# Scores of q and of grad_out in PSUM tiles of their own, and exp one slot earlier, in a decode attention with its gradients

## The chip, the cores and the metric

One core of a Trainium2 chip. The metric is the device time of one execution in microseconds (us), the median of the timed runs. "TensorE" (PE in the profile) does the matmuls and transposes, "VectorE" (DVE) and "ScalarE" (ACT) the elementwise work, "GpSimd" (POOL) issues the stores, "SyncE" (SP) the loads. 16 DMA engines move the data between HBM and SBUF.

## The reference

For 64 heads (2 x 32) there is one query q of 128 numbers, 8192 keys k and values v of 128 numbers each, and the gradient grad_out of the output. All are bf16. What is computed is the output of attention and its three gradients:

```python
def fwd(q, k, v):
    scores = jnp.einsum("bhqd,bhkd->bhqk", q, k) * D ** -0.5
    p = softmax(scores, axis=-1)
    return jnp.einsum("bhqk,bhkd->bhqd", p, v)

out, vjp = jax.vjp(fwd, q, k, v)
return (out, *vjp(grad_out))          # out, dq, dk, dv
```

k and v are read (2 MB a head each), dk and dv are written (2 MB a head each). For each head: s = k q and dp = v grad_out are two columns of 8192 numbers; p is the softmax of the scaled s; dS = p (dp - sum(p dp)); dk is dS times q and dv is p times grad_out, row by row.

## The kernel before, in words

A head's k and v lie in SBUF as 64 tiles (NT) of 128 rows, so that 8192 keys are 128 partitions x 64 columns. They are handled in chunks of 16 tiles (CH): four chunks of k, then four of v, so that a head has eight slots (SL). The main loop (L344) goes through the slots of 64 heads and two more heads' worth of slots for what lags behind, 528 in all; `pin` keeps the instructions of each engine in the order in which they are written.

In slot s of head i TensorE gets this, in this order: 16 transposes of chunk s into a PSUM tile `tp` (L144), which ScalarE copies to SBUF as `ev` (L146, 128 x 2048); 16 matmuls of the head before, which accumulate its output from v (slots 0 to 3, L276, `oacc`) or its dq from k (slots 4 to 7, L292, `qacc`); and 16 matmuls of one column each that give the scores of the chunk of the slot before from its `ev` (L156). The first four chunks give s, the last four dp.

Between these stand the few steps of the softmax. After the scores of chunk 3, in slot 4, VectorE takes the maximum of s by partition (L168, `mp`); in slot 5 TensorE transposes it (L172, into mT) and VectorE takes the maximum of all (L174, `gm`); in slot 6 TensorE spreads it over the partitions (L178, into mb) and VectorE scales it (L181, `negm`). In slot 7, behind the copy of chunk 7, ScalarE computes exp (L191, `E_f`, with the row sums), and VectorE casts it (L201, `E_bf`), which the matmuls of L276 need in slot 0 of the next head. In slot 0 of the next head VectorE multiplies E_f with dp and sums (L207), in slot 1 the sums are spread (L221, into lsum) and dS is made (L243).

VectorE's large work is the outer products (L324, `ob`), four pieces of dv and four of dk a head, which lag by one to two heads. When `ob` is full GpSimd issues its store (L336).

The buffers: kt and vt have three each, so the load of v of head i+1 (L111) waits until the accumulation L276 of head i-2 is done, and the load of k (L106) until L292 of head i-2 is done. `ob` has two for dk and two for dv. In PSUM, `tp` has two buffers, `ps_m` two. `sdpw` (L131) is one tile of 64 + 64 + 128 + 1 + 2 fp32 columns in one bank, with two buffers, and holds s, dp, mT, mb and lsum of a head side by side. The framework puts in a wait wherever an instruction writes a tile that another engine still reads, by the tile and not by its columns.

Of the kernel before, what the change touches and what calls it, by code (L numbers as in the profile page):

```python
# [12 lines left out]
F32 = mybir.dt.float32  # L13
# [5 lines left out]
def kernel(  # L19
# [14 lines left out]
    P = nc.NUM_PARTITIONS  # L34
# [3 lines left out]
    NT = Sk // P  # L38
    assert NT * P == Sk and NT == 4 * CH
    NCH = NT // CH  # L40
# [10 lines left out]
    work = ctx.enter_context(tc.tile_pool(name="work", bufs=3))  # L51
    outp = ctx.enter_context(tc.tile_pool(name="outp", bufs=2))
    ps_tp = ctx.enter_context(tc.tile_pool(name="ps_tp", bufs=2, space=bass.MemoryType.PSUM))
    ps_sdp = ctx.enter_context(tc.tile_pool(name="ps_sdp", bufs=2, space=bass.MemoryType.PSUM))
    ps_m = ctx.enter_context(tc.tile_pool(name="ps_m", bufs=2, space=bass.MemoryType.PSUM))


# [24 lines left out]

    dqT = const.tile([P, BH], BF16)
    o_all = const.tile([1, BH, D], BF16)

    MT0 = 2 * NT
    MB0 = MT0 + P
    LS0 = MB0 + 1
    SDPW = LS0 + 2

    class Head:
        pass
# [1 line left out]
    heads = [Head() for _ in range(BH)]  # L94

    def load_k(i):
        h = heads[i]
        h.kt = kvp.tile([P, NT, D], BF16, tag="K", name="kt")
        if i == 0:
            for c in range(NCH):  # L100
                load_eng.dma_start(
                    out=h.kt[:, c * CH : (c + 1) * CH, :],
                    in_=k_v[i, :, c * CH : (c + 1) * CH, :],
                )
        else:
            load_eng.dma_start(out=h.kt[:], in_=k_v[i])  # L106

    def load_v(i):
        h = heads[i]
        h.vt = kvp.tile([P, NT, D], BF16, tag="V", name="vt")  # L110
        load_eng.dma_start(out=h.vt[:], in_=v_v[i])  # L111

    def broadcast(i):

        h = heads[i]
        qbp = ps_m.tile([P, 2, D], F32, tag="m", name="qbp")
        pin(
            nc.tensor.matmul(  # L118
                qbp[:],
                lhsT=ident_bf[:BH, i : i + 1].to_broadcast([BH, P]),  # L120
                rhs=qd_nat[:],
                start=True,
                stop=True,
            )
        )
        h.qb = work.tile([P, 2, D], BF16, tag="qb", name="qb")
        pin(nc.vector.tensor_copy(out=h.qb[:], in_=qbp[:]))  # L127

    def begin(i):
        h = heads[i]  # L130
        h.sdpw = ps_sdp.tile([P, SDPW], F32, tag="sdp", name="sdpw")  # L131
        h.s = h.sdpw[:, 0:NT]
        h.dp = h.sdpw[:, NT : 2 * NT]
        h.mT = h.sdpw[0:1, MT0 : MT0 + P]
        h.mb = h.sdpw[:, MB0 : MB0 + 1]
        h.lsum = h.sdpw[:, LS0 : LS0 + 2]

    def transpose_chunk(i, c):
        h = heads[i]
        src = h.kt if c < NCH else h.vt  # L140
        n0 = (c % NCH) * CH
        tp = ps_tp.tile([P, CH, P], BF16, tag="tp", name="tp")
        for t in range(CH):
            pin(nc.tensor.transpose(tp[:, t, :], src[:, n0 + t, :], ident_bf[:]))  # L144
        ev = evp.tile([P, CH, P], BF16, tag="ev", name="ev")
        pin(nc.scalar.copy(out=ev[:], in_=tp[:]))  # L146
        return ev

    def score_chunk(i, c, ev):
        h = heads[i]  # L150
        w = c // NCH
        dst = h.s if w == 0 else h.dp
        n0 = (c % NCH) * CH
        for t in range(CH):
            pin(
                nc.tensor.matmul(  # L156
                    dst[:, n0 + t : n0 + t + 1],
                    lhsT=ev[:, t, :],
                    rhs=qdT[:, w, i : i + 1],
                    start=True,  # L160
                    stop=True,
                )
            )

    def max_part(i):
        h = heads[i]
        h.mp = work.tile([P, 1], F32, tag="mp", name="mp")
        pin(nc.vector.reduce_max(out=h.mp[:], in_=h.s, axis=AX.X))  # L168

    def max_all(i):  # L170
        h = heads[i]
        pin(nc.tensor.transpose(h.mT, h.mp[:], ident_f[:]))  # L172
        h.gm = work.tile([1, 1], F32, tag="gm", name="gm")
        pin(nc.vector.reduce_max(out=h.gm[:], in_=h.mT, axis=AX.X))  # L174

    def max_spread(i):
        h = heads[i]
        pin(nc.tensor.matmul(h.mb, lhsT=ones_f[0:1, :], rhs=h.gm[:], start=True, stop=True))  # L178
        h.negm = work.tile([P, 1], F32, tag="negm", name="negm")
        pin(  # L180
            nc.vector.tensor_scalar(  # L181
                out=h.negm[:], in0=h.mb, scalar1=-scale, scalar2=None, op0=ALU.mult
            )
        )

    def expo(i):
        h = heads[i]
        h.E_f = work.tile([P, NT], F32, tag="E_f", name="E_f")
        h.ld = work.tile([P, 2], F32, tag="ld", name="ld")
        pin(  # L190
            nc.scalar.activation(  # L191
                out=h.E_f[:],
                in_=h.s,
                func=ACT.Exp,
                bias=h.negm[:],
                scale=scale,
                accum_out=h.ld[:, 0:1],
            )
        )
        h.E_bf = work.tile([P, NT], BF16, tag="E_bf", name="E_bf")  # L200
        pin(nc.vector.tensor_copy(out=h.E_bf[:], in_=h.E_f[:]))  # L201

    def weigh(i):
        h = heads[i]
        junk = work.tile([P, NT], BF16, tag="junk", name="junk")
        pin(
            nc.vector.tensor_tensor_reduce(  # L207
                out=junk[:],
                in0=h.E_f[:],
                in1=h.dp,  # L210
                scale=1.0,
                scalar=0.0,
                op0=ALU.mult,
                op1=ALU.add,
                accum_out=h.ld[:, 1:2],
            )
        )
# [51 lines left out]
    def acc_o(i, c):  # L269

        h = heads[i]
        if c == 0:
            h.oacc = ps_m.tile([1, D], F32, tag="m", name="oacc")
        for n in range(c * CH, (c + 1) * CH):
            pin(
                nc.tensor.matmul(  # L276
                    h.oacc[:],
                    lhsT=h.E_bf[:, n : n + 1],
                    rhs=h.vt[:, n, :],
                    start=(n == 0),  # L280
                    stop=(n == NT - 1),
                )
            )

    def acc_dq(i, c):

        h = heads[i]
        if c == 0:
            h.qacc = ps_m.tile([P, 1], F32, tag="m", name="qacc")
        for n in range(c * CH, (c + 1) * CH):  # L290
            pin(
                nc.tensor.matmul(  # L292
                    h.qacc[:],
                    lhsT=h.kt[:, n, :],
                    rhs=h.dS_bf[:, n : n + 1],
                    start=(n == 0),
                    stop=(n == NT - 1),
                )
            )

    def end_o(i):
        h = heads[i]
        pin(
            nc.scalar.activation(  # L304
                out=o_all[:, i, :], in_=h.oacc[:], func=ACT.Copy, scale=h.rl[0:1, :]
            )
        )

    def end_dq(i):
        h = heads[i]  # L310
        pin(
            nc.scalar.activation(
                out=dqT[:, i : i + 1], in_=h.qacc[:], func=ACT.Copy, scale=h.rls[:]
            )
        )
# [28 lines left out]
    for g in range(SL * (BH + 2)):  # L344
        i, s = divmod(g, SL)
        live = i < BH
        one = 0 <= i - 1 < BH
        two = 0 <= i - 2 < BH
        if s == 0 and i + 1 < BH and i >= 1:
            load_v(i + 1)  # L350
            load_k(i + 1)
        if live:
            if s == 0:
                begin(i)
            if s == 1:
                broadcast(i)
            ev = transpose_chunk(i, s)

        if live and s == 5:
            max_all(i)  # L360
        if live and s == 7:
            expo(i)
        if one and s == 1:
            normalise(i - 1)
        if one:
            if s < NCH:
                acc_o(i - 1, s)
            else:
                acc_dq(i - 1, s - NCH)
        if live and s == 6:  # L370
            max_spread(i)
        if prev is not None:
            score_chunk(*prev)
        prev = (i, s, ev) if live else None
        if live and s == 4:
            max_part(i)
        if one and s == 0:
            weigh(i - 1)
        if one and s == NCH - 1:
            end_o(i - 1)  # L380
        if one and s == SL - 1:
            end_dq(i - 1)
        if one and 2 <= s < 6:
            outer(i - 1, 1, s - 2)
        if one and s >= 6:
            outer(i - 1, 0, s - 6)
        if two and s < 2:
            outer(i - 2, 0, s + 2)
# [37 lines left out]
```

## Time and profile before

| what | us |
|---|---|
| median of the 2 timed runs | 1506.98 (1506.83 to 1507.13) |
| the profiled execution | 1496.58 |
| its span, first to last instruction | 1494.8 |
| TensorE busy (87%) | 1303.5 |
| ScalarE busy (67%) | 995.7 |
| VectorE busy (50%) | 747.4 |

The profiled execution is one run with the hardware profiler on; its rows and its span belong to that run, 0.7% under the median of the others. Busy times are sums over the instructions of one engine. The mean granted clock of TensorE was 0.824 of its full speed. One head takes about a sixty-fourth of the span.

### The profile page before, as it was taken

Reading aid. Unit: us, or ns where it says so; the run is one execution under the profiler, and the core shown is the slowest. Engines: PE = TensorE matmul, PEld = TensorE weight load, DVE = VectorE, ACT = ScalarE, POOL = GpSimd, SP = SyncE. Lnnn points to the kernel's source line nnn. Section 1 sums busy time; section 2 is a strip of 40 time slices with the busy share of each in tenths; the row PEclk is TensorE's granted clock in tenths of the full one; section 3 lists DMA queues with packets and bytes.
Section 4 is the critical chain, followed back from the end, with each engine's and each line's share of the span. In section 5 each row is a group of like instructions: output and inputs, shape, how many; then the busy total and the mean of one; then the engine's idle time right before and its main releaser. Section 6 shows DMA issues by size and latency. Waiting matters only on the chain.

```text
span 1494.8 us, 53368 instructions
## 1 busy us (share of the span) xinstructions
PE 1303.5 (87%) x24963; PEld 1211.7 (81%) x24963; DVE 747.4 (50%) x1412; ACT 995.7 (67%) x769; POOL 69.2 (5%) x136
## 2 busy tenths in 40 slices
PE   7898898988988988988889889898898898988984
PEld 6888787888888878878878888888887787888884
DVE  1454454554554554555445555555455444554554
ACT  6666766667767667667676676676666666667762
POOL 0000000000000000000000000000000000000000
PEclk9887887888878788788788887888788778888986
DMA  8898989999999999899899999999989989899966
GB/s 339 338 372 363 371 356 360 358 368 373 379 376 369 376 376 367 357 378 359 350 354 377 376 370 384 368 374 372 372 347 383 359 344 365 349 377 384 384 278 255
DMA packets 37760, 540.37 MB, mean 361 GB/s; under 512 B 4385, under 2 KB 4385, under 8 KB 4897
## 3 DMA queue, kind: packets, MB, share of 16 engines
q1 hardware_dynamic: 19106, 268.51, 46.0%
q0 software_dynamic: 18432, 268.44, 45.2%
q8 instruction: 195, 3.19, 0.8%
q14 instruction: 27, 0.22, 0.0%
HBM read 268.47 MB, written 268.47 MB: 359 GB/s over the span
## 4 chain that ended last, share of the span: by engine, by line
PE 59%; issue 25%; ACT 7%; DVE 6%; POOL 1%; DMA 1%; SPq 0%; POOLq 0%; ACTq 0%
PE tp L144 26%; PE oacc L276 16%; PE sdpw L156 13%; ACT ev L146 6%; DVE ob L324 4%; PE qacc L292 2%; POOL out_dram L336 1%; PE sdpw L178 1%; ACT E_f L191 1%; PE qbp L118 1%; DMA vt<-in_v_dram 1%; DVE mp L168 1%; PE sdpw L221 1%; DVE gm L174 1%; DVE negm L181 1%
## 5 line engine op out<-in xcount | busy, mean ns | idle before, releaser
L146 ACT COPY ev<-tp 128x2048 bf16<-128x2048 bf16 x512 | 948.7, 1866 | 472.1 <-PE tp L144 470.3
L324 DVE TENSOR_TENSOR ob<-qb,pair 128x2048 bf16<-128x2048 bf16 x512 | 611.6, 1216 | 0.0
L156 PEld LDWEIGHTS <-ev 128*128 128x128 bf16 x8192 | 258.0, 98 | 200.3 <-issue 174.1
L156 PE MATMUL sdpw<-qdT,ev 128*128 128x1 bf16 x8192 | 283.3, 164 | 154.6 <-ACT E_f L191 121.6
L144 PE MATMUL tp<-ident_bf,kt 128*128 128x128 bf16 x4096 | 342.2, 250 | 2.1 <-DMA kt<-in_k_dram 2.1
L276 PE MATMUL oacc<-vt,E_bf 128*1 128x128 bf16 x4096 | 332.4, 246 | 0.0
L144 PEld LDWEIGHTS <-kt 128*128 128x128 bf16 x4096 | 295.1, 114 | 14.5 <-issue 10.0
L144 PE MATMUL tp<-ident_bf,vt 128*128 128x128 bf16 x4096 | 295.3, 229 | 7.3 <-issue 5.3
L276 PEld LDWEIGHTS <-E_bf 128*1 128x1 bf16 x4096 | 277.5, 95 | 26.4 <-issue 12.2
L144 PEld LDWEIGHTS <-vt 128*128 128x128 bf16 x4096 | 251.6, 103 | 9.5 <-issue 7.5
L292 PE MATMUL qacc<-dS_bf,kt 128*128 128x1 bf16 x4096 | 142.2, 164 | 7.0 <-issue 7.0
L292 PEld LDWEIGHTS <-kt 128*128 128x128 bf16 x4096 | 136.0, 97 | 9.0 <-issue 8.3
L336 POOL DMA_DIRECT2D out_dram<-ob x128 | 68.2, 532 | 1414.6 <-DVE ob L324 1410.6
L168 DVE TENSOR_REDUCE mp<-sdpw 128x1 f32<-128x64 f32 x64 | 14.4, 225 | 214.9 <-PE sdpw L156 214.9
L207 DVE CUSTOM_DVE_ANT_0 junk<-E_f,sdpw 128x64 bf16<-128x64 f32 x64 | 14.2, 221 | 206.0 <-PE sdpw L156 206.0
L201 DVE CAST E_bf<-E_f 128x64 bf16<-128x64 f32 x64 | 12.5, 196 | 199.5 <-ACT E_f L191 199.5
L181 DVE TENSOR_SCALAR negm<-sdpw 128x1 f32<-128x1 f32 x64 | 10.1, 158 | 84.0 <-PE sdpw L178 84.0
L127 DVE CAST qb<-qbp 128x256 bf16<-128x256 f32 x64 | 26.7, 418 | 4.1 <-PE qbp L118 4.1
L304 ACT ACTIVATE o_all<-oacc,rl 1x128 bf16<-1x128 f32 x64 | 22.6, 353 | 8.9 <-PE oacc L276 8.9
L178 PE MATMUL sdpw<-gm,ones_f 1*128 1x1 f32 x128 | 25.0, 261 | 0.9 <-issue 0.9
L221 PE MATMUL sdpw<-ld,ones_f 128*128 128x2 f32 x128 | 24.1, 257 | 0.3 <-DVE ld L207 0.3
L118 PE MATMUL qbp<-qd_nat,ident_bf 64*128 64x256 bf16 x64 | 22.9, 358 | 0.0
(33 smaller groups left out, 249.2 us busy)
## 6 DMA issues: line engine op xcount, KB each, us to landing
out_dram<-ob POOLq DMA_DIRECT2D x128, 2048.0 KB, 10.3
vt<-in_v_dram SPq DMA_DIRECT2D x64, 2048.0 KB, 13.0
kt<-in_k_dram SPq DMA_DIRECT2D x63, 2048.0 KB, 12.6
kt<-in_k_dram SPq DMA_DIRECT2D x4, 512.0 KB, 4.4
qd_nat<-in_q_dram SPq DMA_DIRECT2D x1, 16.0 KB, 2.0
qd_nat<-in_grad_out_dram SPq DMA_DIRECT2D x1, 16.0 KB, 2.0
out_dram<-o_all SPq DMA_DIRECT2D x1, 16.0 KB
out_dram<-dqn SPq DMA_DIRECT2D x1, 16.0 KB, 7.5
```

The source lines that it names most:

```text
L118: nc.tensor.matmul(qbp[:], lhsT=ident_bf[:BH, i : i + 1].to_broadcast([BH, P]), rhs=qd_nat[:], start=True, stop=True,)
L127: pin(nc.vector.tensor_copy(out=h.qb[:], in_=qbp[:]))
L144: pin(nc.tensor.transpose(tp[:, t, :], src[:, n0 + t, :], ident_bf[:]))
L146: pin(nc.scalar.copy(out=ev[:], in_=tp[:]))
L156: nc.tensor.matmul(dst[:, n0 + t : n0 + t + 1], lhsT=ev[:, t, :], rhs=qdT[:, w, i : i + 1], start=True, stop=True,)
L168: pin(nc.vector.reduce_max(out=h.mp[:], in_=h.s, axis=AX.X))
L178: pin(nc.tensor.matmul(h.mb, lhsT=ones_f[0:1, :], rhs=h.gm[:], start=True, stop=True))
L221: pin(nc.tensor.matmul(h.lsum, lhsT=ones_f[:], rhs=h.ld[:], start=True, stop=True))
L276: nc.tensor.matmul(h.oacc[:], lhsT=h.E_bf[:, n : n + 1], rhs=h.vt[:, n, :], start=(n == 0), stop=(n == NT - 1),)
L292: nc.tensor.matmul(h.qacc[:], lhsT=h.kt[:, n, :], rhs=h.dS_bf[:, n : n + 1], start=(n == 0), stop=(n == NT - 1),)
L324: nc.vector.tensor_tensor(out=h.ob[:, n0 : n0 + CH, :].rearrange("p n (e t) -> p n e t", t=2), in0=h.qb[:, w, :] .rearrange("p (e t) -> p ...
L336: store_eng.dma_start(out=dst[i], in_=h.ob[:])
```

## The change

The tile `sdpw` with two buffers becomes two tiles with one buffer each, in banks of their own: one with s, mT and mb, which a head takes in slot 1, and one with dp and lsum, which it takes in slot 5. exp and the cast behind it are issued in slot 6, right behind the scaling of the maximum, and so ahead of the copy of chunk 7 on ScalarE and ahead of the scores of chunk 5 in the written order.

```diff
-    ps_sdp = ctx.enter_context(tc.tile_pool(name="ps_sdp", bufs=2, space=bass.MemoryType.PSUM))
+    ps_sdp = ctx.enter_context(tc.tile_pool(name="ps_sdp", bufs=1, space=bass.MemoryType.PSUM))
...
-    MT0 = 2 * NT
-    MB0 = MT0 + P
-    LS0 = MB0 + 1
-    SDPW = LS0 + 2
...
-    def begin(i):
-        h = heads[i]
-        h.sdpw = ps_sdp.tile([P, SDPW], F32, tag="sdp", name="sdpw")
-        h.s = h.sdpw[:, 0:NT]
-        h.dp = h.sdpw[:, NT : 2 * NT]
-        h.mT = h.sdpw[0:1, MT0 : MT0 + P]
-        h.mb = h.sdpw[:, MB0 : MB0 + 1]
-        h.lsum = h.sdpw[:, LS0 : LS0 + 2]
+    def begin_s(i):
+        h = heads[i]
+        sw = ps_sdp.tile([P, NT + P + 1], F32, tag="s", name="sw")
+        h.s = sw[:, 0:NT]
+        h.mT = sw[0:1, NT : NT + P]
+        h.mb = sw[:, NT + P : NT + P + 1]
+
+    def begin_dp(i):
+        h = heads[i]
+        dpw = ps_sdp.tile([P, NT + 2], F32, tag="dp", name="dpw")
+        h.dp = dpw[:, 0:NT]
+        h.lsum = dpw[:, NT : NT + 2]
...
         if live:
-            if s == 0:
-                begin(i)
             if s == 1:
+                begin_s(i)
                 broadcast(i)
+            if s == NCH + 1:
+                begin_dp(i)
             ev = transpose_chunk(i, s)
...
-        if live and s == 7:
-            expo(i)
...
         if live and s == 6:
             max_spread(i)
+            expo(i)
         if prev is not None:
             score_chunk(*prev)
```

## Rows read from the trace of the kernel before

**Rows 1.** The page: busy us and share of two engines; the span in 40 slices.

```profile
PE 1303.5 (87%) x24963; PEld 1211.7 (81%) x24963; DVE 747.4 (50%) x1412; ACT 995.7 (67%) x769; POOL 69.2 (5%) x136
...
DMA  8898989999999999899899999999989989899966
GB/s 339 338 372 363 371 356 360 358 368 373 379 376 369 376 376 367 357 378 359 350 354 377 376 370 384 368 374 372 372 347 383 359 344 365 349 377 384 384 278 255
```

**Rows 2.** The waits of the whole run: us in total, times, longest us.

```profile
PE sdpw L156 <- ACT E_f L191: 121.6, 64, 2.3
...
PE sdpw L156 <- DVE negm L181: 16.0, 64, 0.3
PE sdpw L156 <- DVE gm L174: 15.1, 64, 0.4
...
PE tp L144 <- DMA kt<-in_k_dram: 2.1, 1, 2.1
```

**Rows 3.** Timeline of PE: start us, us, line, operation, [idle before <-releaser].

```profile
706.31 1.05 PE L144 MATMUL tp<-ident_bf,vt 128*128 128x128 bf16 x16
...
709.04 0.56 PE L156 MATMUL sdpw<-qdT,ev 128*128 128x1 bf16 x16 [0.25 <-DVE negm L181]
709.46 1.87 PE L144 MATMUL tp<-ident_bf,vt 128*128 128x128 bf16 x16
...
713.64 0.57 PE L156 MATMUL sdpw<-qdT,ev 128*128 128x1 bf16 x16 [1.91 <-ACT E_f L191]
...
715.87 1.86 PE L276 MATMUL oacc<-vt,E_bf 128*1 128x128 bf16 x16
...
720.14 1.05 PE L276 MATMUL oacc<-vt,E_bf 128*1 128x128 bf16 x16
```

**Rows 4.** Timeline of ACT and DVE in the same head.

```profile
707.45 1.86 ACT L146 COPY ev<-tp 128x2048 bf16<-128x2048 bf16 x1 [0.24 <-PE tp L144]
...
708.83 0.16 DVE L181 TENSOR_SCALAR negm<-sdpw 128x1 f32<-128x1 f32 x1 [1.84 <-PE sdpw L178]
...
711.42 1.86 ACT L146 COPY ev<-tp 128x2048 bf16<-128x2048 bf16 x1 [2.10 <-PE tp L144]
...
713.18 0.32 ACT L191 ACTIVATE E_f<-sdpw,negm 128x64 f32<-128x64 f32 x1
713.39 0.20 ACT L191 ACTIVATION_READ_ACCUMULATOR E_f<-sdpw,negm 128x1 f32 x1
```

**Rows 5.** Stretches: us, busy by engine, then PEclk, DMA share, GB/s.

```profile
709.60:713.00 3.40, 2.13 (x32) 2.07 (x31) 0.52 (x1) 1.58 (x1) 0.00 (x0) 0.50 0.95 328
...
717.00:721.00 4.00, 4.00 (x58) 3.53 (x56) 2.41 (x8) 1.77 (x2) 0.00 (x0) 0.69 1.05 446
721.00:724.00 3.00, 3.00 (x70) 2.66 (x68) 2.98 (x6) 2.31 (x2) 0.53 (x1) 1.00 0.21 82
...
0.00:60.00 60.00, 46.60 (x812) 42.56 (x813) 17.81 (x42) 37.98 (x27) 2.28 (x10) 0.86 0.82 330
60.00:1440.00 1380.00, 1222.95 (x23522) 1137.39 (x23520) 701.82 (x1324) 936.56 (x724) 63.76 (x120) 0.83 0.94 368
...
12.00:32.00 20.00, 14.89 (x250) 13.59 (x248) 1.93 (x11) 13.38 (x10) 0.00 (x0) 0.83 1.01 429
1404.00:1432.00 28.00, 25.58 (x485) 23.70 (x483) 15.25 (x34) 19.13 (x14) 1.06 (x2) 0.85 0.99 394
```

**Rows 6.** The page, DMA queues: packets, MB, packet time as share of 16 engines.

```profile
q1 hardware_dynamic: 19106, 268.51, 46.0%
q0 software_dynamic: 18432, 268.44, 45.2%
q8 instruction: 195, 3.19, 0.8%
```

**Rows 7.** The page, DMA issues: count, KB each, median us to landing.

```profile
out_dram<-ob POOLq DMA_DIRECT2D x128, 2048.0 KB, 10.3
```

## The prediction

> **What bounds the kernel now.** I read the page's engine rows and slices first, then the waits, the timeline of one head in mid-run, and last the DMA rows by stretches.
>
> No engine is busy for the whole span: TensorE 1303.5 us of 1494.8 (87%), ScalarE 995.7 (67%). The DMA row stands at 8 or 9 tenths all the way, with slices from 338 to 384 GB/s [rows 1]. So two things stand close together: TensorE with its waits, and the 16 DMA engines. Which one sets the pace is read from who waits. TensorE has waited for a load of k a single time, 2.1 us [rows 2], so after the start no load was late: TensorE and its waits are the pace, and the DMA engines follow.
>
> What TensorE waits for: the score matmuls of L156 wait for the exp of L191 64 times, once a head, 121.6 us in all (1.90 us a head), for the scaled maximum of L181 another 16.0 us, and for the maximum of L174 15.1 us [rows 2]. All of these are waits for a tile and not for data: the matmuls in question write dp columns, while exp, L174 and L181 read s, mT and mb, which share the tile `sdpw` with dp. In the timeline the pair that counts is seen at 711 to 714 us. The copy of chunk 7 starts at 711.42 and takes 1.86 us, exp follows at 713.18, and the 16 score matmuls of chunk 6, whose own copy had been ready since about 709.3, start at 713.64 after 1.91 us of idling [rows 3, 4].
>
> There is a second loss beside it. The 16 transposes that started at 706.31 took 1.05 us, those at 709.46 took 1.87 us, and the accumulation at 715.87 took 1.86 us against 1.05 at 720.14 [rows 3]; the granted clock of 709.6 to 713.0 is 0.50, the 1.2 GHz level, and 1.00 again (2.4 GHz) at 721 to 724 [rows 5]. Ahead of the fall TensorE had idled 0.25 us before the scores at 709.04; the 1.91 us wait lies inside the slow stretch [rows 3].
>
> **The change part by part.**
>
> *Separate tiles for s and dp.* The waits for L191, L174 and L181 lose their reason: nothing writes s between the scores of chunk 3 and the next head. That is 121.6 + 16.0 + 15.1 = 152.7 us of TensorE idle time, 2.39 us a head. What is late next on TensorE is the copy that each score chunk needs in any case; at 1.86 us a copy against one slot of matmuls it is about even, and ScalarE has in all 995.7 / 64 = 15.6 us of work a head, so it is no bound.
>
> *One buffer in place of two.* The scores of chunk 0 now write the same s tile as the head before. Its last reader is exp, which the change issues in slot 6, two slots and more ahead. The first write of dp comes in slot 5; the last readers of the old dp are the weighing in slot 0 and the normalisation in slot 1, more than three slots ahead. A slot is some 1494.8 / 528 = 2.8 us, so I cost this at nothing; the cover is those slots. Were it gone, a wait of up to one slot a head, 64 x 2.8 = 180 us, would come in.
>
> *exp ahead of the copy of chunk 7.* Same two instructions, 0.32 + 0.20 us [rows 4]. ScalarE now idles 2.10 us between the copy of chunk 6 and that of chunk 7 [rows 4], and they fall into that gap. exp has to wait for `negm`, which came at 708.83 plus 0.16, 0.3 us before the copy of chunk 6 ended at 709.31 [rows 4]; so it waits for nothing, and what is queued behind it, copy 7, is held up by at most 0.52 us. If transposes 7 come sooner than today the whole 0.52 us may show on copy 7, but TensorE needs that copy only after a full set of transposes and the first accumulation of the next slot. I take 0; if the cover goes it is 64 x 0.52 = 33 us. The gain side is already counted above. No DMA issue is moved: the SP waits of the loads hang on L276 and L292, the store issues on L324, and all of them just come earlier as the head gets shorter.
>
> *The clock.* With the waits gone the 1.2 GHz stretches should shorten. Bounds: none of the present loss comes back (0), or each 1.87 us set of transposes falls to 1.05 us, and accumulations of slot 0 likewise, some 3 x 0.8 = 2.4 us a head. I need no value, because of the next part.
>
> *What TensorE alone would give.* 1494.8 - 152.7 = 1342.1 us at the present clock, less if the clock recovers. That is not to be had, since the DMA engines come first.
>
> *The DMA engines.* Packets of the three queues took 46.0 + 45.2 + 0.8 = 92.0% of 16 engines' span [rows 6], 1375 us, and the steady part (60 to 1440 us) has a share of 0.94 at 368 GB/s [rows 5]. The idle part is seen once a head, as at 721 to 724 us: share 0.21, 82 GB/s [rows 5]. A shorter head closes that gap and no more; after it the loads are late and TensorE waits for kt. So the term is how fast the engines move data when always fed, in both directions. The ends: 368 (today's mean, gaps included), and 429 GB/s, the stretch 12 to 32 us, where loads run alone [rows 5]. The nearest row is 1404 to 1432 us, over a head long, loads and stores mixed, share 0.99: 394 GB/s [rows 5]. I take 394. The steady part becomes 1380 x 368 / 394 = 1289 us, 91 us less.
>
> *Start and end.* The first 60 us have a share of 0.82 [rows 5], 11 us of idle engines, part of it before the first load; I take a quarter, 3 us. The end, after the last load, is TensorE's and VectorE's; one wait and some slow clock less there, 3 us.
>
> Sum: 91 + 3 + 3 = 97 us. The profiled execution took 1496.58 us (span 1494.8), so 1399.6 us. The median of the timed runs, 1506.98, stands 0.7% over it; carried over as a factor, 1399.6 x 1506.98 / 1496.58 = 1409 us.
>
> A rule that speaks against the change: the Trainium skill, DMA: Bandwidth & Descriptors, section Bandwidth (Where 436 GB/s comes from), says that transfers between HBM and SBUF are bound by the HBM side at about 358 GB/s a core. By that rule alone the 540.37 MB would need 1509 us as an estimate, so nothing could be gained. The trace disagrees: 429 GB/s over 20 us and 446 at 717 to 721 [rows 5].
>
> **The rivals.**
>
> *A. The DMA engines do better when always fed.* The mixed stretch at 717 to 721 us ran at 446 GB/s, the losses sit where one transfer gives way to another (328 at 709.6 to 713.0) [rows 5]. If most of these go, 415 GB/s: 1380 x 368 / 415 = 1224, 156 us off, with the 6 us 1334.6, times 1.0069 = 1344 us. Against it: the change adds nothing that orders transfers.
>
> *B. Half of it.* TensorE, now waiting for a late kt at the start of a head, falls to 1.2 GHz there and loses some of the wait again, and the DMA gap closes only in half: 45 + 3 us, 1449 us, 1459 for the runs. For it: the fall of the clock today follows idle time. Against it: slots 0 to 3 hold twice the 128-column matmuls of slots 4 to 7, and TensorE has slack behind the DMA engines.
>
> *C. No change.* The engines are at their limit already at 368 GB/s and the gap at 721 to 724 only moves; 1507 us. For it: the mean share of 0.94. Against it: share 0.99 with 394 GB/s over 28 us [rows 5]. That the wait stays (another dependence on exp holds the same matmuls) would end here too; nothing in the code holds them.
>
> *D. Slower.* Loads and stores, now always in flight together, run at the rate of a changeover all the time, 328 GB/s: 1380 x 368 / 328 = 1548, 168 us more, about 1676 us for the runs. Stores that now land in 10.3 us [rows 7] would then hold VectorE at the reuse of `ob`. It decides once the fed rate falls below 361 (368 less 2%). Against it: 414 to 446 mixed is on record too.
>
> **How the numbers follow.** The forecast 0.57 (1380 to 1440), A 0.20 (1330 to 1380), B 0.10 (1440 to 1477), C 0.10 (1477 to 1537), D 0.03. The range reaches from about A's value to about B's: 1343 to 1460. Faster by over 2%, about what a measurement of this kernel tells from no change, means under 1476.8 us: forecast, A and B, 0.87; within 2% C, 0.10; slower D, 0.03.
>
> **What would show it.** Right: no wait of L156 for L191, L174 or L181; exp between the copies of chunks 6 and 7; a DMA share of 0.98 or more in the steady part at 390 to 400 GB/s; a new wait of the transposes of L144 for kt, 1 to 4 us in most heads; SP's waits for L276 and L292 shorter in total. Wrong: a share still near 0.94 (TensorE or ScalarE is then the bound, look at the clock), or a share near 1 with less than 380 GB/s. If waits for E_f stay, the first step is wrong.

## The result, and the profile after

The changed kernel takes 1337.67 us (median of 2 runs, 1336.71 and 1338.63) against 1506.98: a ratio of 0.8877, 95% interval 0.8838 to 0.8915. Faster, as forecast, but by more than forecast: 1409 was predicted, and the range ended at 1343. The profiled execution is the run of 1336.71 us, its span 1334.9 us.

The page of the changed kernel: engines, the DMA slices, the queues, the landing times (they answer to [rows 1], [rows 6] and [rows 7]).

```profile
PE 1219.1 (91%) x24963; PEld 1135.2 (85%) x24963; DVE 744.9 (56%) x1412; ACT 989.2 (74%) x769; POOL 69.5 (5%) x136
...
DMA  9999999999999999999999999999999999999977
...
q1 hardware_dynamic: 19106, 268.51, 49.3%
q0 software_dynamic: 18432, 268.44, 48.6%
q8 instruction: 195, 3.19, 0.9%
...
out_dram<-ob POOLq DMA_DIRECT2D x128, 2048.0 KB, 18.5
```

The DMA row is full until the last two slices, and a store now lands 18.5 us after its issue, where it was 10.3. The steady part (columns as in [rows 5]) moves 409 GB/s at a share of 1.00, against 368 at 0.94:

```profile
60.00:1300.00 1240.00, 1152.25 (x23586) 1073.29 (x23587) 704.80 (x1336) 933.50 (x725) 64.50 (x121) 0.90 1.00 409
0.00:60.00 60.00, 50.64 (x991) 46.63 (x991) 20.87 (x49) 44.88 (x33) 2.82 (x11) 0.94 0.95 377
```

The waits of TensorE, all that are over 3 us (columns as in [rows 2]):

```profile
PE tp L145 <- DMA kt<-in_k_dram: 28.6, 28, 3.3
PE dpw L157 <- issue: 23.2, 23, 2.5
PE tp L145 <- issue: 19.9, 20, 1.8
PE qacc L293 <- issue: 16.6, 15, 2.4
```

TensorE waits for exp, L175 or L182 no more. In their place stand loads of k that come late, 28 times, and "issue", idle time without a releaser. A head of the same stretch as in [rows 3] and [rows 4], first ScalarE, then TensorE:

```profile
711.36 1.87 ACT L147 COPY ev<-tp 128x2048 bf16<-128x2048 bf16 x1 [1.67 <-PE tp L145]
713.12 0.32 ACT L192 ACTIVATE E_f<-sw,negm 128x64 f32<-128x64 f32 x1
...
714.51 1.87 ACT L147 COPY ev<-tp 128x2048 bf16<-128x2048 bf16 x1 [0.98 <-PE tp L145]
```

```profile
709.65 0.18 PE L157 MATMUL dpw<-qdT,ev 128*128 128x1 bf16 x1 [1.13 <-issue]
709.69 1.58 PE L145 MATMUL tp<-ident_bf,vt 128*128 128x128 bf16 x16
...
712.55 1.87 PE L145 MATMUL tp<-ident_bf,vt 128*128 128x128 bf16 x16
714.22 0.61 PE L293 MATMUL qacc<-dS_bf,kt 128*128 128x1 bf16 x16
714.69 0.56 PE L157 MATMUL dpw<-qdT,ev 128*128 128x1 bf16 x16
```

exp (L192) runs right behind the copy of chunk 6, and the copy of chunk 7 starts after 0.98 us of idling, when its transposes are done, so exp holds nothing up. The scores of chunk 6 (714.69) follow L293 without a gap. The 1.2 GHz level is still there in this head (transposes of 1.87 us at 712.55), now behind an idle 1.13 us at 709.65. The mean granted clock went from 0.824 to 0.900.

### The profile page after: what moved, and what is told of

It reads as the page before. It is cut to its first block, busy times and chain, and to the rows that moved or that the text cites. A ratio compares the mean times of both kernels' runs of the same rounds, so it can differ in the third digit from the quotient of the medians.

```text
span 1334.9 us, 53368 instructions
## 1 busy us (share of the span) xinstructions
PE 1219.1 (91%) x24963; PEld 1135.2 (85%) x24963; DVE 744.9 (56%) x1412; ACT 989.2 (74%) x769; POOL 69.5 (5%) x136
## 3 DMA queue, kind: packets, MB, share of 16 engines
q0 software_dynamic: 18432, 268.44, 48.6%
## 4 chain that ended last, share of the span: by engine, by line
PE 49%; issue 27%; DMA 22%; POOL 1%; DVE 0%; ACT 0%; SPq 0%; POOLq 0%; ACTq 0%
PE tp L145 22%; DMA kt<-in_k_dram 21%; PE oacc L277 12%; PE sw L157 5%; PE dpw L157 4%; PE qacc L293 4%; POOL out_dram L337 1%; DMA vt<-in_v_dram 1%; PE sw L179 1%; PE qbp L113 1%; PE dpw L222 0%; PE sw L173 0%; ACT ev L147 0%; DVE ob L325 0%; SPq L96 0%
## 5 line engine op out<-in xcount | busy, mean ns | idle before, releaser
L145 PE MATMUL tp<-ident_bf,kt 128*128 128x128 bf16 x4096 | 314.2, 237 | 30.8 <-DMA kt<-in_k_dram 28.6
L277 PE MATMUL oacc<-vt,E_bf 128*1 128x128 bf16 x4096 | 306.1, 234 | 0.9 <-issue 0.8
L145 PEld LDWEIGHTS <-kt 128*128 128x128 bf16 x4096 | 267.3, 107 | 44.0 <-DMA kt<-in_k_dram 31.3
L157 PEld LDWEIGHTS <-ev 128*128 128x128 bf16 x8192 | 243.2, 97 | 62.4 <-issue 32.1
L277 PEld LDWEIGHTS <-E_bf 128*1 128x1 bf16 x4096 | 254.6, 90 | 26.3 <-issue 9.9
L157 PE MATMUL dpw<-qdT,ev 128*128 128x1 bf16 x4096 | 145.0, 164 | 24.1 <-issue 23.2
L293 PE MATMUL qacc<-dS_bf,kt 128*128 128x1 bf16 x4096 | 141.8, 164 | 16.6 <-issue 16.6
L293 PEld LDWEIGHTS <-kt 128*128 128x128 bf16 x4096 | 134.6, 97 | 18.8 <-issue 18.0
L157 PE MATMUL sw<-qdT,ev 128*128 128x1 bf16 x4096 | 140.8, 164 | 1.2 <-ACT ev L147 0.8
L169 DVE TENSOR_REDUCE mp<-sw 128x1 f32<-128x64 f32 x64 | 14.4, 225 | 205.3 <-PE sw L157 205.3
L202 DVE CAST E_bf<-E_f 128x64 bf16<-128x64 f32 x64 | 12.5, 195 | 83.8 <-ACT E_f L192 83.8
L182 DVE TENSOR_SCALAR negm<-sw 128x1 f32<-128x1 f32 x64 | 10.2, 159 | 78.3 <-PE sw L179 78.3
L179 PE MATMUL sw<-gm,ones_f 1*128 1x1 f32 x128 | 24.9, 260 | 1.0 <-issue 1.0
L192 ACT ACTIVATE E_f<-sw,negm 128x64 f32<-128x64 f32 x64 | 21.3, 332 | 4.6 <-DVE negm L182 4.5
## 6 DMA issues: line engine op xcount, KB each, us to landing
out_dram<-ob POOLq DMA_DIRECT2D x128, 2048.0 KB, 18.5
```

Of the source, the lines that this page charges most:

```text
L157: nc.tensor.matmul(dst[:, n0 + t : n0 + t + 1], lhsT=ev[:, t, :], rhs=qdT[:, w, i : i + 1], start=True, stop=True,)
L192: nc.scalar.activation(out=h.E_f[:], in_=h.s, func=ACT.Exp, bias=h.negm[:], scale=scale, accum_out=h.ld[:, 0:1],)
L277: nc.tensor.matmul(h.oacc[:], lhsT=h.E_bf[:, n : n + 1], rhs=h.vt[:, n, :], start=(n == 0), stop=(n == NT - 1),)
L293: nc.tensor.matmul(h.qacc[:], lhsT=h.kt[:, n, :], rhs=h.dS_bf[:, n : n + 1], start=(n == 0), stop=(n == NT - 1),)
```

## The experiments

**Which edit does it.** The first run has the separate tiles alone: exp goes back behind the copy of chunk 7.

```diff
+        if live and s == 7:
+            expo(i)
...
         if live and s == 6:
             max_spread(i)
-            expo(i)
```

> Separate one-buffer tiles for s and dp, exp left behind the copy of chunk 7. Theory (the false wait on the shared tile is the whole cost, and the DMA engines set the end once it is gone): the scores of chunk 6 write dp alone and wait for nothing, exp is ready by slot 0 either way; 1335 to 1345 us, DMA share in the steady part 0.99 or more. Rival (the place of exp matters too): the cast behind exp comes too late for the accumulation of slot 0, a wait of some 0.5 to 1 us a head comes back; 1360 to 1420 us.

Measured: 1340.98 us, ratio 0.8923 (0.8861 to 0.8985), the same as the full change within the intervals. The theory holds. Of the rival one part is seen, a wait of the accumulation for the cast behind exp, in 19 heads. The time does not show it, and the waits for late loads are shorter by about as much (17.9 us in place of 28.6):

```profile
PE tp L145 <- DMA kt<-in_k_dram: 17.9, 18, 2.2
...
PE oacc L277 <- DVE E_bf L202: 13.4, 19, 1.8
```

The second run has exp's new place alone, in the kernel before:

```diff
-        if live and s == 7:
-            expo(i)
...
         if live and s == 6:
             max_spread(i)
+            expo(i)
```

> exp in slot 6, s and dp still in one shared tile with two buffers. Theory: the scores of chunk 5, behind exp in the written order, now write the tile that exp reads and wait for it and so for the copy of chunk 6 ahead of it; the wait of some 1.9 us a head is only moved by a slot; 1470 to 1540 us, waits of L156 for L191 near 100 us or over. Rival (the place of exp alone does it): the wait falls to under 40 us in all and the time to under 1400 us.

Measured: 1416.53 us, ratio 0.9441 (0.9381 to 0.9501). The wait is as the theory said, the time is not; it lies on neither side's numbers.

```profile
PE 1270.3 (89%) x24963; PEld 1190.0 (84%) x24963; DVE 745.2 (52%) x1412; ACT 997.2 (70%) x769; POOL 69.2 (5%) x136
...
PE sdpw L156 <- ACT E_f L191: 97.4, 64, 1.9
PE sdpw L156 <- DVE gm L174: 15.0, 64, 0.4
```

The span is 1421.8, 73.0 us less. 24 us are shorter waits for exp and 16 the wait for `negm`, which is gone; the other 33 are TensorE's busy time, 1303.5 to 1270.3, at a clock of 0.853 against 0.824. The same number of matmuls took less time because less of it lay in the slow level. So a wait in another place can cost less than its length suggests, and the theory had left that out. The two edits do not add: with the tiles apart, exp's place is worth nothing that shows.

**What bounds each kernel.** A quarter of the bytes is taken away from both, by leaving out the stores of dk.

```diff
-        if c == NCH - 1:
+        if c == NCH - 1 and (w == 1 or i == 0):
             dst = dk_v if w == 0 else dv_v
```

> The changed kernel without the stores of dk for all heads but the first; all else stays, a quarter of the moved bytes is left out. Theory (the DMA engines set the end after the change): the time falls well below 1337 us, to what TensorE and ScalarE need, about 18 to 19 us a head, 1190 to 1260 us, with no waits of the transposes for kt. Rival (TensorE and its clock are still the bound, the full DMA share is a coincidence): within 2% of 1337 us.

> The kernel before without the stores of dk for all heads but the first, a quarter of the moved bytes left out. Theory (before the change TensorE with its waits set the pace): hardly faster, 1470 to 1507 us, with the waits of L156 for L191 still near 120 us. Rival (the DMA engines bounded the kernel before too): the time falls by over 5%, below 1430 us.

Measured: 1188.33 us (2 us under the theory's range) and 1474.02 us, each of one run. The changed kernel loses 149 us with a quarter of its bytes, the kernel before 33 of 1507. So after the change the time hangs on the transfers, and before it TensorE with its waits set the pace. In the changed kernel without the stores TensorE is busy 96% at a clock of 0.978:

```profile
PE 1136.7 (96%) x24963; PEld 1062.9 (90%) x24963; DVE 743.3 (63%) x1412; ACT 978.9 (82%) x769; POOL 35.7 (3%) x73
```

Little of what the stores of dk cost the changed kernel is waiting for late data. Of the 148 us of span that go, 82 are TensorE's busy time (1219.1 to 1136.7, at the higher clock), some 35 its idle time without a releaser, and 26 its waits for late k. So the stores act on TensorE by more than one path, and these runs do not tell the paths apart.

**How fast the transfers can be.** Loads and stores run alone; the main loop is replaced by this one (lines taken out are not shown):

```diff
+    for i in range(BH):
+        if i + 1 < BH and i >= 1:
             load_v(i + 1)
             load_k(i + 1)
...
+        store_eng.dma_start(out=dv_v[i], in_=full[:])
+        store_eng.dma_start(out=dk_v[i], in_=full[:])
```

> Loads and stores of the changed kernel alone, on their two queues, the stores from one tile of zeros; transposes, scores, softmax, accumulations and outer products are left out. Theory (loads and stores that are both always pending run together at some 410 to 420 GB/s, and this sets the end of the changed kernel): 1285 to 1325 us, so the changed kernel has only its start and end above it. Rival (the compute engines' traffic slows the transfers): 1240 to 1265 us, near the 429 GB/s of loads alone. Second rival (the rate of the changed kernel is still not the fed rate): under 1230 us.

and the same with `store_eng = nc.sync` and the two stores put between the loads:

> The same transfers alone, but stores issued on the loads' queue, a load and a store in turn; all compute is left out. Theory (what costs is the handover from one transfer to another, and two fed queues hide it): slower than with two queues, 1340 to 1450 us, at 375 to 405 GB/s. Rival (handovers cost nothing, the two directions just share the engines): the same time as with two queues within 1%.

Measured: 1255.16 and 1256.14 us. The first is in the range of the first rival (its cause, the compute engines' traffic, is put to the test further below), the second is its own rival's: handovers between transfers cost nothing as long as the queue is fed. The page of the run on two queues:

```profile
q1 hardware_dynamic: 19106, 268.51, 50.2%
q0 software_dynamic: 18432, 268.44, 50.0%
```

Share times span is the packet time of the two queues: 100.2% of 1253.4 = 1256 us. For the same bytes it was 91.2% of 1494.8 = 1363 us in the kernel before and 97.9% of 1334.9 = 1307 us after the change. So the same bytes have no fixed price. By the packets' own times in the traces the median packet of 16 KB took 611 ns in all three runs; what differs is how many took over 700 ns: 2 of 32641 with the transfers alone, 12.5% in the kernel before, 5.8% after the change. What makes these packets dearer is the question for the runs below.

**Stores spread, and stores on the loads' queue.**

```diff
-        if c == NCH - 1:
-            dst = dk_v if w == 0 else dv_v
-            store_eng.dma_start(out=dst[i], in_=h.ob[:])
+        dst = dk_v if w == 0 else dv_v
+        store_eng.dma_start(out=dst[i, :, n0 : n0 + CH, :], in_=h.ob[:, n0 : n0 + CH, :])
```

> The changed kernel with each 2 MB store issued as four stores of 512 KB, one behind each outer product. Theory (the transfers set the end, and stores that are spread over the head keep both queues pending): 1310 to 1345 us, the last store shorter by up to 10 us at the end. Rival (each start of a store costs the transfers of the other queue): four times the starts, 1345 to 1420 us.

Measured: 1365.14 us, ratio 0.9055 (0.9016 to 0.9093): slower than the full change, in the rival's range. But the edit changes more than the number of starts: a quarter of a store comes in packets of 4 KB where they were of 16 KB, 73728 of them on the stores' queue in place of 18432. So the run does not show that it is the starts that cost.

```diff
-    store_eng = nc.gpsimd
+    store_eng = nc.sync
```

> The changed kernel with the stores issued on the queue of the loads. Theory (one queue hands over from transfer to transfer, and a load issued behind a store waits for that store's outer products too): 1370 to 1500 us, share of the transfers below 0.99 or a rate below 400 GB/s. Rival (which queue the stores are on does not matter): 1330 to 1350 us.

Measured: 1333.42 us, ratio 0.8840 (0.8797 to 0.8884). The rival holds: the queue does not matter. It is the fastest by median, but its interval overlaps that of the change, so no gain over the change can be told.

**Which engine, or which rhythm.** To the kernel of transfers alone one stream of compute was added, tied to no transfer (one diff of each run, with the views of the operands left out):

```diff
+    for _ in range(1000):
+        pin(nc.vector.tensor_tensor(out=sink, in0=src, in1=pr, op=ALU.mult))
...
+    for _ in range(650):
+        pin(nc.scalar.copy(out=sink[:], in_=tp[:]))
...
+    for _ in range(1250):
+        for t in range(CH):
+            pin(nc.tensor.transpose(tp[:, t, :], src[:, t, :], ident_bf[:]))
```

> Loads and stores alone as in the run with transfers only, and beside them 1000 outer products of the kernel's form on VectorE, on tiles that no transfer touches; all else of the computation is left out. Theory 1 (VectorE's traffic in SBUF slows the transfers): 1300 us or over, packets at a mean of 635 ns or more. Rival (ScalarE or TensorE does, or it is the rhythm of the transfers and no engine): within 1% of 1255 us.

> The same transfers, and beside them 650 copies of 128x2048 from PSUM to SBUF on ScalarE; all else is left out. Theory 2 (ScalarE's writes slow the transfers): 1300 us or over. Rival: within 1% of 1255 us.

> The same transfers, and beside them 20000 transposes on TensorE from a tile in SBUF; all else is left out. Theory 3 (TensorE's reads of weights and columns slow the transfers): 1300 us or over (should TensorE itself take longer than the transfers, the packets' mean tells: 635 ns or more). Rival: packets at 611 ns, transfers done within 1% of 1255 us.

Measured: 1272.02, 1256.00 and 1302.19 us. The first lies between the theory's range and the rival's; VectorE's own 1000 products are busy for 1232.5 of its 1270.3 us, and the steady rate is 431 GB/s as without them. ScalarE's copies change nothing. Beside TensorE the time passes the theory's 1300, but the packets don't: (48.4 + 48.6)% of 1300.4 = 1261 us. Its stretches show 427 GB/s beside the transposes, and a tail at the end (columns: TensorE, its weight loads, VectorE, GpSimd, clock, share, GB/s):

```profile
100.00:1100.00 1000.00, 1000.00 (x17914) 1000.00 (x17912) 0.00 (x0) 52.60 (x99) 1.00 1.01 427
...
1250.00:1260.00 10.00, 0.00 (x0) 0.00 (x0) 0.00 (x0) 0.00 (x0) 0.50 0.57 245
...
1280.00:1290.00 10.00, 0.00 (x0) 0.00 (x0) 0.00 (x0) 0.00 (x0) 0.50 0.07 28
```

A share of 0.57, then 0.07, means that some of the 16 engines, and at the last about one, had fallen behind. All three streams at once:

> Loads and stores alone, and beside them all three streams of the single runs at once: outer products on VectorE, copies on ScalarE, transposes on TensorE, none of them tied to a transfer; the rest of the computation is left out. Theory (engines' traffic slows the packets, but only several engines together): packet time, the two queues' share times the span, over 1300 us against 1256 without compute. Rival (rhythm): packet time within 1.5% of 1256 us.

Measured: 1305.99 us, packet time (48.5 + 48.3)% of 1304.2 = 1262 us: the rival, within 1.5% of 1256. Traffic in SBUF by these streams does not make fed packets dearer. The next runs are about the rhythm. In the first of them each store takes the tile that was loaded (`in_=heads[i].vt[:]` and `kt[:]` in place of `full[:]`):

> The same transfers without any compute, but each store takes the tile that was loaded, so a store starts when its load has landed and a load when a store three before has; all computation is left out. Theory 4 (it is the rhythm: a transfer that starts on an idle queue beside one in flight slows both for some us): 1290 us or over, with packets over 700 ns at the starts. Rival (an engine's traffic): 1255 to 1275 us, packets at 611 ns.

Measured: 1255.67 us, against the theory. The steady share is 1.01 at 431 GB/s, so this chain kept both queues fed and says nothing of queues that run dry. The paced kernel lets them run dry (an excerpt of its loop; `piece` makes a quarter of `ob`, and issues the store behind the last):

```diff
...
+        for _ in range(fill[sl]):
+            product(sink[:])
+        if one and sl == 3:
+            pin(nc.vector.tensor_copy(out=seen[:, 0:1], in_=heads[i - 1].vt[:, 0, 0:1]))
+        if one and sl == 7:
+            pin(nc.vector.tensor_copy(out=seen[:, 1:2], in_=heads[i - 1].kt[:, 0, 0:1]))
+        if one and 2 <= sl < 6:
+            piece(i - 1, 1, sl - 2)
+        elif one and sl >= 6:
+            piece(i - 1, 0, sl - 6)
...
```

> Loads and stores in the rhythm of the kernel before: VectorE alone runs 19 products a head, some 23.3 us; stores of dv and dk are issued behind the products of slots 5 and 1, loads are released in slots 3 and 7; transposes, scores, softmax and accumulations are left out. The time is VectorE's, some 1500 us, and says nothing; the packet time does. Theory (rhythm: a queue that runs dry and starts again costs): packet time of the two queues 1330 to 1370 us, as in the kernel before (91.2% of 1494.8 = 1363). Rival (traffic of the compute engines): 1256 to 1275 us.

> The same rhythm, and beside it 20000 free transposes on TensorE in the first 1120 us or so; the rest is left out. Theory (rhythm alone): packet time as in the paced run without them within 1.5%. Rival (rhythm and TensorE's reads or its instructions together): over 30 us more packet time than in the paced run.

The queues and the steady part of the paced run (columns as in the last rows):

```profile
q1 hardware_dynamic: 19106, 268.51, 46.7%
q0 software_dynamic: 18432, 268.44, 45.6%
...
60.00:1440.00 1380.00, 0.00 (x0) 0.00 (x0) 1373.60 (x1315) 66.44 (x125) 1.00 0.94 373
```

Measured: packet time 92.3% of 1466.6 = 1354 us, and with TensorE's transposes beside it 92.0% of 1468.7 = 1351 us. The paced run has almost nothing of the kernel but its timing, and it has the share and nearly the rate of the kernel before (0.94 and 368). Of its 16 KB packets 14.0% took over 700 ns. So the rhythm is enough to make the packets as dear as they were, and TensorE's stream adds nothing. VectorE, which sets the pace, is busy for 99% of the paced run; beside fed queues its products changed nothing, but no run was paced without them.

## Why the prediction was wrong, point by point

*What bounds the kernel before: right.* TensorE with its waits set the pace; without a quarter of the bytes it hardly moved.

*Separate tiles, one buffer, exp's place: right.* TensorE's waits for L191, L174 and L181 are gone, no new wait for a tile came with the single buffers, and exp waited for `negm` 6 times, 4.5 us in all. The split alone gives the whole gain.

*The transfers set the end: right in the main.* The share is 1.00, and 149 us go without the stores of dk. Of the signs I named, the share and the shorter waits of SP came (for the accumulation of the output 848.5 to 713.3 us). The late kt came in 28 heads, at about 1 us, not in most: 28.6 us in all, and idle time without a releaser, which the prediction did not have, is twice that (59.7 us in its three rows).

*"I take 394": this term failed.* The forecast let the 507.8 MB of the steady part (368 x 1380) move at 394 GB/s, in 1289 us. They moved at 409, in 1242 us: 138 us off in place of 91, 47 us of the miss. The row 1404 to 1432 us had a share of 0.99, but its transfers had been started by the old rhythm, one by one as compute let them go, and the packets of that rhythm are dearer: 1354 us of packet time in the paced run, 1256 when both queues are always fed. Removing the wait did not only close the gaps, it made the packets themselves cheaper, 1363 to 1307 us. A share near 1 in the kernel before was therefore not the rate of fed engines. The run with exp's place alone says the same: a steady share of 0.98 at 386 GB/s, with TensorE still waiting 97.4 us for exp. Rival A was near with its rate (415), and its band of 1330 to 1380 us holds the measured time, but not for its reason: handovers cost nothing in a fed queue (1256.14 against 1255.16 us). "The change adds nothing that orders transfers" was the wrong argument against it: the change takes away what had spaced them.

*Start and end, 3 + 3 us: too small.* Together 159.9 - 138 = 22 us came off. The first 60 us moved 377 GB/s against 330, some 7 us' worth at 409; the rest is in the last stretch and was not taken apart.

*The factor 1.0069: wrong, 9 us.* The distance between the profiled run and the median was the spread between runs and no property of the profile. The kernel before took 1493 to 1516 us in the sets timed beside the experiments.

*The rule of the 358 GB/s* (the Trainium skill, DMA: Bandwidth & Descriptors, Bandwidth): no run on this one core agrees. Transfers alone ran at 431 GB/s for over 1000 us. The prediction left out that the same section, under its table, ties the figure of about 358 to both cores of a pair streaming; no run here has two cores.

*The rivals.* C and D fell with the share of 1.00 at 409. B's clock drop was there, but in the head shown it follows 1.13 us of idling without a releaser and not a late kt. What it cost was not measured apart.

What stays open: the 1307 us of the changed kernel are still 51 over 1256. That some of the rhythm is left there is likely, since its loads still wait for TensorE to release their buffers (713.3 and 492.8 us of SP's waits for L277 and L293), but no run took this apart. Why packets are dearer in this rhythm, and which packets of a transfer, was not found.

## What to carry to other kernels

When a stall is removed and the transfers become the bound, the rate to put in the sum is not that of the busiest stretch of the stalled kernel. In this case that stretch, 394 GB/s, was the lower end and a kernel of the same transfers alone, 431 GB/s, the upper; the changed kernel came out between, at 409. Two values that share a PSUM tile make each writer wait for the other's reader: look there before moving instructions, since the split alone did here what both edits did.

## What was not expected of the hardware

TensorE's idle time without a releaser ("issue") grew from 7.0 + 5.3 us in the two largest rows of the kernel before to 23.2 + 19.9 + 16.6 us in the changed one, and without the stores of dk it is 12.2 us in its largest row. Instructions come by DMA too (the queue q8, 195 packets in both kernels), and the packets' times in the traces say that this is what TensorE waits for: 61 of its 62 idle times of this kind over 0.15 us in the changed kernel, and all 26 in the kernel before, end 1.2 to 1.7 us after the end of an instruction packet, where about 7% would by chance. Why there are more of them now is not shown. The share of the DMA engines alone does not say it: the run with exp's place alone has 0.98 and only 6.3, 4.5 and 3.3 us in these rows. Beside 20000 transposes some engines ended some 45 us after the bulk of the transfers, though the packet time of the two queues grew by 5 us only; that run has 156 instruction packets which the transfers alone lack, and whether these sit on the engines that ended last is not shown.
